# A recurrence and a two-layer network on one core: the first steps' instructions placed one by one, with six more idle products

## The chip, the cores and the metric

The kernel runs on one core of a Trainium2 chip. That core has TensorE (matrix products, PE in the profile), VectorE (DVE), ScalarE (ACT), GpSimd (POOL) and SyncE (SP), each with its own instruction queue; SyncE and GpSimd mostly issue transfers here. The metric is the device time of one execution in microseconds. Several executions of a kernel give a median.

## The reference

```python
# attention block: B, H, S, D = 4, 8, 768, 48
f = 1.0 / (1.0 + np.exp(-f_logit))
for t in range(S):
    state = f[:, :, t, :, None] * state + np.einsum('bhd,bhe->bhde', k[:, :, t], v[:, :, t])
    y[:, :, t] = np.einsum('bhd,bhde->bhe', q[:, :, t], state)
# x: y as (B*S, H*D) = (3072, 384)
h = x @ w_in                                            # 384 -> 2048
g = np.maximum(h, 0.0) + alpha * np.minimum(h, 0.0)
out = g @ w_out                                         # 2048 -> 384
```

A gated linear recurrence runs over 768 tokens for each of 4 x 8 heads; its output goes token by token through a two-layer network with a leaky gate.

## The kernel before, in words

The sequence is cut into six chunks of 128 tokens, and the four batches into two pairs. That makes twelve steps, numbered 0 to 11: step 0 is chunk 0 of the first pair, step 1 chunk 0 of the second, step 2 chunk 1 of the first, and so on. Each step has two halves. The attention half turns the recurrence of one chunk into products: it takes the sigmoid of the gates, makes running products of them, forms products of scaled queries and keys inside blocks of 32 tokens (in smaller parts: lags within four tokens, quads, halves), puts those masked into a matrix `A`, and multiplies by the values and by the state carried from the chunk before. The network half multiplies the step's 256 tokens (tile `xT`) by `w_in` (`ph`), gates the result, and multiplies by `w_out`.

In the attention half the names are these. `loaded` issues the loads of f, q, k and v, for step 0 on SyncE's queue and for all others on GpSimd's. `lagging` and `lagged_all` make the gates and the lagged copies `qd` (lines 329 to 346). `scanned` copies operands (lines 363 to 366), `scanned_all` runs two scans on VectorE (373, 374). `gated`, `keyed`, `started`, `ended`, `carried` and `begun` scale queries and keys (380 to 418). The products are `raw` (line 582, lags), `qu` (line 591 for quads, line 681 for the half blocks of steps 0 and 1), `off` (566, between blocks of 32), `pk` (713, transposes of the keys), `pd` (539, the state's increment), `py` (614, the output) and `xt` (738, which packs the output of step 0 into 128 rows). VectorE copies the masked parts of `raw` (599) and `qu` (702) into `ad`; ScalarE copies the rest (688), then `ad` into `A` (606), `off` into `A` (573), the keys (719), the increment (556), the output (729), and `xT` (747).

The weights arrive as 64-bit numbers in 16 pieces of some 767 KB on SyncE's queue. ScalarE takes each apart in two instructions (lines 281 and 282), VectorE puts the halves together in a third (291). The words `a0` to `a7` are the load and ScalarE's two instructions for a piece of `w_in`, `w0` to `w7` VectorE's instruction for it; `b0` to `b7` and `v0` to `v7` are the same for `w_out`. `W`, `Y` and `Z` with a number derive sums and splits of the weights for another form of the network, which later steps use.

In the first step TensorE also runs products whose result is not used: fourteen at the start (`IDLE`), six (`BEFORE`, words `0I0` to `0I5`) and eight (`BEHIND`, words `0J0` to `0J7`). The profile shows them at line 935, two records each.

The order of all this is written out by hand in `ORDER_WORDS`. A word names a step and a part: `0r1` is step 0, `raw` of the second batch of the pair; `0Na3` is step 0, network, product 3 of the first layer. A word that runs issues all the instructions of its part, on whatever engines they are for. In the kernel before, the order of words binds TensorE, VectorE and ScalarE; the queues of GpSimd and SyncE are ordered by the scheduler:

```python
    with tc.manual_schedule(engines={mybir.EngineType.PE, mybir.EngineType.DVE, mybir.EngineType.Activation}):
...
        for key in ORDER:
            run[key]()
```

## Time and profile before

| | us |
|---|---|
| median of 3 runs | 595.74 |
| lowest, highest | 594.69, 597.52 |
| span of the profiled execution | 592.1 |
| TensorE busy in that span | 580.1 |
| VectorE busy | 505.7 |
| ScalarE busy | 300.4 |
| GpSimd busy | 68.4 |

The profiled execution shows its span and no other time. In the profile PE is TensorE's products, PEld its weight loads (which overlap products), PEclk the clock that TensorE was granted (1.00 is full). A timeline's row gives the start from the beginning of the span, the duration, the engine, the line, and what is written from what; runs of equal instructions are put together (x128). In brackets is the idle time of the engine ahead of the row and what ended it. A row of windows gives the stretch, its length, each engine's busy time with its instructions, the clock, the share of the DMA engines, and GB/s.

### The profile page before, as it was taken

The numbers are of one execution on the slowest core, as the hardware profiler recorded it, in microseconds if no ns is written. First come the engines' busy times: TensorE is split into PE (matmuls) and PEld (weight loads), VectorE is DVE, ScalarE is ACT, GpSimd is POOL, SyncE is SP. The second block draws the span as 40 slices with busy tenths as digits, with TensorE's granted clock in tenths as the row PEclk, the third lists the DMA queues.
The fourth block names the chain that finished last, engine by engine and source line by source line (L and its number), as shares of the span: only waits on it lengthen the run. The fifth ranks groups of instructions, "written<-read, shape, count | busy, mean of one in ns | idle before, by whom it ended". The sixth has DMA issues, their size and how long they took to land.

```text
span 592.1 us, 18853 instructions
## 1 busy us (share of the span) xinstructions
PE 580.1 (98%) x8200; PEld 527.9 (89%) x8200; DVE 505.7 (85%) x1027; ACT 300.4 (51%) x561; POOL 68.4 (12%) x114
## 2 busy tenths in 40 slices
PE   8799999999999999999999999999999999999997
PEld 6678767899899999999999999899899999899997
DVE  7889799899999989899989889989989979966243
ACT  5697973461472473483382374374275355443230
POOL 9110010000101101111111101101100100100100
PEclk9689999999999999999999999999999999999999
DMA  9959212612523823724624614722732731611300
GB/s 299 356 160 348 98 22 63 172 30 86 123 86 91 191 78 89 172 65 105 169 60 106 153 68 106 164 74 85 148 110 81 152 110 54 112 44 30 80 2 27
DMA packets 69443, 67.57 MB, mean 114 GB/s; under 512 B 44688, under 2 KB 58640, under 8 KB 69360
## 3 DMA queue, kind: packets, MB, share of 16 engines
q1 hardware_dynamic: 59744, 37.16, 22.1%
q0 software_dynamic: 8880, 28.84, 19.2%
q8 instruction: 64, 1.05, 0.7%
q10 hardware_dynamic: 736, 0.37, 0.2%
q14 instruction: 19, 0.16, 0.1%
HBM read 44.99 MB, written 13.50 MB: 99 GB/s over the span
## 4 chain that ended last, share of the span: by engine, by line
PE 80%; issue 10%; DMA 4%; ACT 3%; DVE 3%; POOL 1%; POOLq 0%; ACTq 0%; DVEq 0%
PE ph L831 36%; PE pa L886 9%; PE pd L886 5%; PE pf L886 5%; PE pe L886 5%; PE pb L886 5%; PE pc L886 4%; PE py L614 3%; PE qu L591 3%; PE raw L582 3%; DMA w_out_raw<-in_w_out 2%; PE pd L539 1%; PE off L566 1%; DVE ad L451 1%; DMA f<-in_fT 1%
## 5 line engine op out<-in xcount | busy, mean ns | idle before, releaser
L831 PE MATMUL ph<-xT,w_in_sb 128*128 128x256 f32 x612 | 137.1, 380 | 0.2 <-DMA xT<-y 0.2
L831 PEld LDWEIGHTS ph<-xT,w_in_sb 128*128 128x128 f32 x612 | 115.1, 190 | 16.9 <-issue 0.9
L854 ACT ACTIVATE gate<-ph 128x512 f32<-128x512 f32 x96 | 54.6, 594 | 134.4 <-PE ph L831 127.5
L859 DVE SCALAR_TENSOR_TENSOR gate<-gate,om,ph 128x256 f32<-128x256 f32 x192 | 81.0, 476 | 25.6 <-ACT gate L854 25.1
L886 PE MATMUL pa<-w_out_sb,gate 128*128 128x192 f32 x352 | 61.7, 329 | 0.0
L880 DVE TENSOR_TENSOR gate<-gate 128x512 f32<-128x512 f32 x88 | 57.6, 690 | 3.2 <-PE pb L886 2.4
L886 PEld LDWEIGHTS pa<-w_out_sb,gate 128*128 128x128 f32 x352 | 57.1, 190 | 0.5
L599 DVE COPY_PREDICATED ad<-mraw,raw 128x256 f32<-128x256 int32 (+1 forms) x96 | 42.7, 445 | 8.9 <-PE raw L582 6.2
L451 DVE COPY_PREDICATED ad<-mquad,qu 128x224 f32<-128x224 int32 (+6 forms) x140 | 42.2, 302 | 6.8 <-PE qu L591 1.7
L606 ACT COPY A<-ad 32x256 f32<-32x256 f32 x96 | 38.7, 403 | 11.8 <-DVE ad L451 10.4
L440 DVE TENSOR_TENSOR scores<-scores,fs 128x768 f32<-128x768 f32 (+5 forms) x60 | 37.4, 623 | 1.6
L844 ACT ACTIVATE ph<-ph 128x512 f32<-128x512 f32 x36 | 20.2, 574 | 34.0 <-PE ph L831 25.2
L831 PE MATMUL ph<-xh,hi 128*128 128x256 f32 x216 | 34.4, 295 | 0.0
L831 PE MATMUL ph<-xl,lo 128*128 128x256 f32 x216 | 32.0, 283 | 0.3 <-issue 0.3
L886 PE MATMUL pb<-t,gate 128*128 128x192 f32 x176 | 31.2, 331 | 0.0
L831 PEld LDWEIGHTS ph<-xh,hi 128*128 128x128 f32 x216 | 28.7, 190 | 2.8 <-issue 1.6
L424 ACT COPY A<-q 48x512 f32<-48x512 f32 x44 | 27.2, 617 | 7.8 <-DVE q L398 7.2
L886 PE MATMUL pd<-t,gate 128*128 128x192 f32 x176 | 30.7, 328 | 0.3 <-DVE gate L880 0.3
L886 PE MATMUL pc<-t,gate 128*128 128x192 f32 x176 | 30.6, 327 | 0.0
L886 PE MATMUL pf<-w_out_sb,gate 128*128 128x192 f32 x176 | 30.5, 327 | 0.0
L323 POOL DMA_DIRECT2D vs<-in_v x22 | 13.2, 605 | 149.4 <-PE py L614 149.1
L886 PE MATMUL pe<-w_out_sb,gate 128*128 128x192 f32 x176 | 30.4, 326 | 0.0
(153 smaller groups left out, 1044.0 us busy)
## 6 DMA issues: line engine op xcount, KB each, us to landing
w_out_raw<-in_w_out SPq DMA_DIRECT2D x8, 767.8 KB, 9.6
w_in_raw<-in_w_in SPq DMA_DIRECT2D x8, 767.2 KB, 9.5
q<-in_qT POOLq DMA_DIRECT2D x11, 512.0 KB, 5.1
f<-in_fT POOLq DMA_DIRECT2D x11, 512.0 KB, 5.2
k<-in_kT POOLq DMA_DIRECT2D x11, 512.0 KB, 4.2
turned<-f SPq DMA_DIRECT2D x40, 128.0 KB, 4.4
ksn<-turned SPq DMA_DIRECT2D x10, 512.0 KB, 3.5
out<-o SPq DMA_DIRECT2D x24, 192.0 KB, 1.9
```

What stands on the lines that cost most here:

```text
L424: nc.scalar.copy(A[halves(cc)[1], :, par * HP:(par + 1) * HP, CH * cc:CH * (cc + 1)], x["q3"][rows(par)].rearrange("p (u h c) s t -> p u h ...
L440: nc.vector.tensor_tensor(by_four(us[:, :, UO[m]:UO[m] + 4 * n]), by_four(us[:, :, skip:skip + 4 * n]), spread(fq[:, :, 1:1 + n], n), ALU. ...
L451: nc.vector.copy_predicated(ad[:, u, :, :, 4 * m:DB], mquad[:, lo:lo + n].bitcast(I32).unsqueeze(1).unsqueeze(1).broadcast_to((128, 2, HP, ...
L582: nc.tensor.matmul(raw[DB * j:DB * (j + 1), par, hp * C:hp * C + QW], lhsT=x["k"][r_, g * DB:(g + 1) * DB], rhs=qd[r_, g], start=True, sto ...
L599: nc.vector.copy_predicated(adu[:, :, :, d:4], mraw[:, d, :, d:4].bitcast(I32).unsqueeze(1).broadcast_to((128, H, NB, n)), rv[:, :, QO[d]: ...
L606: nc.scalar.copy(A[s_, u, :, s_], ad[s_, u].rearrange("p r h t -> p (r h) t"))
L831: nc.tensor.matmul(banks[f][:, j * T:(j + 1) * T], lhsT=of[:, kt, 128 * j:128 * (j + 1)], rhs=by[:, kt], start=first_ and kt + j == 0, sto ...
L844: nc.scalar.activation(banks[f], banks[f], AF.Copy, scale=1.0 - 1.0 / EPS)
L854: nc.scalar.activation(to, of, AF.Relu, scale=-1.0)
L859: nc.vector.scalar_tensor_tensor(to[:, j], to[:, j], om[:, m:m + 1], of[:, j], ALU.mult, ALU.add)
L880: nc.vector.tensor_tensor(block(to)[:, p], block(x_)[:, p], block(y_)[:, p], op)
L886: nc.tensor.matmul(banks[to][:, 0:DH], lhsT=block(of)[:, f], rhs=of_w_out(by)[:, f], start=start and f == 0, stop=f == NH - 1, skip_group_ ...
```

## The change

Parts are no longer issued whole. Every part that has several instructions is a generator that yields between them, and a word in the order issues the next instruction of its part; a word therefore stands in the order as many times as its part has instructions. The loads are split into four words (`ef`, `eq`, `ek`, `ev`). GpSimd's and SyncE's queues are now bound to the order too. Tiles that used to be made when a part began are made when first used (`Later`).

With that the order of words is new. From about the middle of step 3 on, each engine's instructions stand in the order they had. (On GpSimd's queue single loads of f, q and k still swap places in later steps.) Ahead of that they are moved, without any being added or dropped but for six idle products (`BEFORE` 6 to 12). In steps 0 and 1 these moves are the ones to follow:

- SyncE: f, q, a piece of `w_in`, k, a piece of `w_out`, two of `w_in`, half of v, a piece of `w_in`, the other half of v, and further pieces. Before: f, q, k, v, v, and then pieces.
- TensorE: `raw`, eleven idle products (five before), `off`, `qu`, `pk`, three idle products, second `qu`, one, `pd`, two, `py`, one, `xt`, second `py`, one, `xt`, `raw` twice, `ph`. Before: `off`, `pk`, `qu`, and both `py` ahead of the first `xt`.
- VectorE: line 386 ahead of 380; the lags (599) of the first half of step 0 mixed in earlier; 663 and 664 ahead of the scaled keys (402, 406).
- ScalarE: eight instructions on weight pieces (six before) ahead of the copies of `off`; behind them the copies of lines 688, 719, 606 and 424, the sigmoid and copies of step 1 (329 to 331) and the copies of line 556 one by one in turn.
- Steps 1, 2 and part of 3: pieces of weights, lags, gates of the network and scans are mixed in another order on all engines; the list of products ahead of the first `ph` is the same but for the idle ones.

The new kernel calls the tile of line 539 `inc` instead of `pd`. The diff, cut to its core:

```diff
-IDLE, BEFORE, BEHIND = 14, 6, 8
+IDLE, BEFORE, BEHIND = 14, 12, 8
...
-0e 1e 0I0 0f 0F 0G 0g 0r1 0h 0i 0m 0p 0j 0r0 0I1 0l 0I2 a0 0R0 0I3 0I4 0I5 0q 0o a1 0k a2 0O 0s 0t w0 0u0 0U0 0R1
-0K0 0H0 1f 0J0 0J1 0J2 w1 0K1 0u1 0J3 0U1 1F 0A0 0d 0D 0H1 0A1 w2 1G 0J4 0J5 0y0 0Y0 b0 0J6 0y1 0x0 0Y1 0M 1g 1i 0J7
-1r0 0x1 1R0 0X a3 1h a4 b1 w3 a5 1m 1r1 w4 1j 0Na0 v0 0Nr0 0Na1 0Na2 1R1 0Na3 a6 0Nc0 w5 0Nr1 0Na4 0Na5 0Nc1 2e 0Nr2
...
+0ef 0f 0f 0eq 0F 0f 0F 0F 0I0 a1 0ek 0F 0F 0g 0g 0g 0g b0 a2 0F 1ef 0r1 a0 0r0 0g 0g 0I1 0G 0G 0I2 0i 0ev 1eq a1 0h b0
+0R0 0j 0m a2 0R0 a3 a2 0p 0p 0p 0p 0I3 0I4 0I5 0I6 0R0 0p 0ev b0 b2 0I7 0R0 0q a1 0q 0l 0I8 0I9 0I10 0I11 a0 a0 0o 0u0
+0l 0U0 0U0 0U0 a4 0O 0O 0s 0k 0s 0R1 0R1 0R1 0O 0J0 0O 0H0 0K0 0R1 0A0 0J1 0H0 0t 0K1 0A0 1ek b3 0J2 1f 0H0 0u1 0J3 1f
+0s b4 w2 v0 0U1 0A0 0U1 0H0 0U1 0t 0H1 0H1 0H1 0d w0 1f 0H1 0D 0A0 0D w1 0A1 0A1 0s 0A1 a5 0J4 2ef 1F 1F 1F 0J5 1F 1F
+0y0 0Y0 1F 0A1 0J6 0x0 0y1 0J7 0M a3 a3 0Y1 0x1 a4 0M a4 0X 0X 0M 1r0 w3 0X 1g 1G 1r1 a7 w4 1g 1p a5 0Na0 1i a5 a6 1g
...
+class Later(dict):
+
+    def __init__(self):
+        self.make = {}
+
+    def __missing__(self, key):
+        self[key] = self.make[key]()
+        return self[key]
+
+
+class Word:
+
+    def __init__(self, part):
+        self.part, self.left = part, None
+
+    def __call__(self):
+        if self.left is None:
+            got = self.part()
+            self.left = got if hasattr(got, "gi_frame") else iter(())
+        next(self.left, None)
...
         nc.scalar.activation(f, f, AF.Sigmoid)
+        yield
         nc.scalar.copy(kr[:, :, 2:3], f[:, :, 3:4])
-        nc.scalar.copy(qd[:, :, 0:DB], q.rearrange("p (g t) -> p g t", t=DB))
+        yield
+        nc.scalar.copy(qd[:, :, 0:DB], x["q"].rearrange("p (g t) -> p g t", t=DB))
...
         for j in range(NJ):
+            if j:
+                yield
             s_ = slice(DB * j, DB * (j + 1))
             nc.scalar.copy(A[s_, u, :, s_], ad[s_, u].rearrange("p r h t -> p (r h) t"))
...
-    with tc.manual_schedule(engines={mybir.EngineType.PE, mybir.EngineType.DVE, mybir.EngineType.Activation}):
+    with tc.manual_schedule(engines={mybir.EngineType.PE, mybir.EngineType.DVE, mybir.EngineType.Activation,
+                                     mybir.EngineType.Pool, mybir.EngineType.SP}):
...
+        run = {key: Word(part) for key, part in run.items()}
         for key in ORDER:
             run[key]()
```

## The prediction

> **What bounds the kernel now.** First the page: busy times, and the chain that ended last.

> ```profile
> span 592.1 us, 18853 instructions
> PE 580.1 (98%) x8200; PEld 527.9 (89%) x8200; DVE 505.7 (85%) x1027; ACT 300.4 (51%) x561; POOL 68.4 (12%) x114
> ...
> PE 80%; issue 10%; DMA 4%; ACT 3%; DVE 3%; POOL 1%; POOLq 0%; ACTq 0%; DVEq 0%
> ```

> TensorE is idle for 12.0 us of the whole span, and it carries the chain. An order of instructions can therefore gain only by closing those gaps, or by changing how long TensorE's own work takes. The second is possible because the granted clock (PEclk) is not full everywhere, as the view by windows shows (span, busy time of each engine with instructions, clock, DMA).

> ```profile
> 5.29:18.94 13.65, 9.75 (x227) 8.06 (x226) 11.51 (x20) 10.34 (x17) 11.24 (x23) 1.00 1.05 366
> 15.50:18.94 3.44, 0.93 (x66) 0.85 (x67) 3.41 (x9) 2.85 (x5) 1.89 (x3) 1.00 1.01 389
> 18.94:32.60 13.66, 13.66 (x242) 10.92 (x241) 11.15 (x26) 8.82 (x19) 0.73 (x1) 0.50 1.03 340
> 32.60:46.25 13.65, 12.33 (x240) 10.28 (x239) 11.68 (x18) 13.33 (x27) 2.65 (x4) 1.00 0.41 106
> 46.25:240.00 193.75, 192.82 (x2586) 167.84 (x2585) 180.13 (x353) 105.02 (x193) 16.07 (x23) 1.00 0.40 115
> ```

> From 18.94 to 32.60 TensorE had half the clock. The 13.65 us before that were 0.71 busy (9.75 of 13.65) and their last 3.44 us only 0.27; the half-clocked window was all busy and full clock came back; the next, 0.90 busy, kept it. From 46.25 to 240 TensorE is idle for 0.93 us in total, while VectorE is busy 180.13 of 193.75 us. So the place to read is the first 46 us; behind it a reordering has 0.93 us to win and a nearly full VectorE to stumble over.

> TensorE's timeline (start, duration, what; last the idle time before it):

> ```profile
> 10.70 1.59 PE L582 MATMUL raw<-qd,k 48*32 48x80 f32 x128 [0.53 <-issue]
> 12.22 2.43 PE L935 MATMUL idle<-ones 128*128 128x256 f32 x10
> 17.47 0.21 PE L566 MATMUL off_0a<-q,kh 48*32 48x32 f32 x1 [2.83 <-DVE kh L402]
> 20.55 1.05 PE L591 MATMUL qu<-scores,k 48*32 48x52 f32 x64
> 21.57 1.97 PE L681 MATMUL qu<-scores 48*128 48x64 f32 x16
> 23.47 2.93 PE L935 MATMUL off_0a<-ones 128*128 128x256 f32 x6
> 34.10 1.15 PE L614 MATMUL py<-A,vs 128*64 128x64 f32 x32 [0.78 <-ACT ad L688]
> 36.42 1.15 PE L614 MATMUL py<-A,vs 128*64 128x64 f32 x32 [0.54 <-ACT y L729]
> 37.50 1.60 PE L738 MATMUL xt<-y,dense 128*128 128x128 f32 x12
> 41.85 0.92 PE L582 MATMUL raw<-qd,k 48*32 48x80 f32 x64
> 42.70 8.04 PE L831 MATMUL ph<-xT,w_in_sb 128*128 128x256 f32 x36
> 58.34 1.04 PE L713 MATMUL pk<-ident,ks 128*128 128x128 f32 x8
> 65.37 0.82 PE L591 MATMUL qu<-scores,k 48*32 48x52 f32 x64
> 66.12 1.11 PE L681 MATMUL qu<-scores 48*128 48x64 f32 x16
> ```

> The first dense product of the network, `ph`, starts at 42.70, and from there TensorE is fed almost without a gap. So the gain is the time by which that first `ph` moves forward, if nothing stalls behind it. The last three rows are the same kinds of product at full clock: `qu` takes 1.11 instead of 1.97 (L681) and 0.82 instead of 1.05 (L591).

> **The change, part by part.**

> *Loads.* On SyncE's queue a 767 KB weight piece now goes ahead of step 0's `k`, and `v` behind three more pieces.

> ```profile
> 1.74 0.47 SPq L313 DMA_DIRECT2D k<-in_kT  x1
> k<-in_kT SPq DMA_DIRECT2D x1, 512.0 KB, 6.2
> ```

> `k` lands at about 1.74 + 6.2 = 7.9; a piece more at 366 GB/s is 2.1 us, so 10.0, and its first reader `raw` starts at 10.70 because it waits for VectorE. Cost 0, with 0.7 us of cover; without that cover at most 2.1 − 0.7 = 1.4. `v` is first needed by the products of line 539, past 25 us. On GpSimd's queue step 1's loads come as f, q, k, each still needed only after 25 us: 0. Later swaps of single loads on that queue cost nothing either: GpSimd and its queue have 1% of the chain.

> *Idle products.* Ten records (five products) took 2.43 us, 0.486 each. There are now eleven between `raw` and `off`, ending at 12.22 + 11 × 0.486 = 17.57; `off` started at 17.47. They fill the 2.83 us gap and delay `off` by 0.1 us at most. The window 5.29 to 18.94 then has 9.75 + 2.83 = 12.6 busy of 13.65, or 0.92, which is what kept the clock in the next window (0.90). I take it that the clock stays full through 18.94. The gap was 2.83 us and the clock still fell. [...]

> *Order up to `qu`.* VectorE's and ScalarE's rows:

> ```profile
> 12.57 1.23 DVE L380 TENSOR_TENSOR scores<-scores,f 128x1024 f32<-128x1024 f32 x1 [0.60 <-ACT scores L365]
> 17.33 0.69 DVE L402 TENSOR_TENSOR ks<-k,ss 128x512 f32<-128x512 f32 x1
> 18.54 1.87 DVE L599 COPY_PREDICATED ad<-mraw,raw 128x256 f32<-128x256 int32 x4
> 20.84 0.67 DVE L664 TENSOR_TENSOR scores<-scores 128x512 f32<-128x512 f32 x1
> 23.64 1.14 DVE L702 COPY_PREDICATED ad<-mhalf,qu 128x224 f32<-128x224 int32 x3
> 22.22 1.25 ACT L424 COPY A<-q 48x512 f32<-48x512 f32 x2 [2.64 <-DVE q L398]
> 24.87 1.06 ACT L688 COPY ad<-qu 16x128 f32<-16x128 f32 x4 [0.81 <-DVE ad L702]
> 25.95 1.06 ACT L329 ACTIVATE f<-f 128x1024 f32<-128x1024 f32 x1
> 27.48 0.65 ACT L330 COPY k<-f 128x256 f32<-128x256 f32 x1 [0.47 <-PE qu L591]
> 28.03 1.04 ACT L331 COPY qd<-q 128x1024 f32<-128x1024 f32 x1
> 29.10 0.58 ACT L719 COPY ksn<-pk_0b 128x512 f32<-128x512 f32 x1
> 29.58 1.64 ACT L606 COPY A<-ad 32x256 f32<-32x256 f32 x4
> 31.97 0.96 ACT L556 COPY vs<-pd 48x384 f32<-48x384 f32 x2 [0.76 <-PE pd L539]
> 35.78 0.58 ACT L729 COPY y<-py 128x512 f32<-128x512 f32 x1
> ```

> L386 moves ahead of L380 and fills the 0.60 us for which VectorE waited; the two `ks` products (17.33 to 18.54, 1.21 us) move behind the operands of `qu`. The last of these, L664, then ends at 20.84 + 0.67 − 0.60 − 1.21 = 19.7 instead of 21.51. The transposes `pk` now follow the first `qu`. Its L681 part runs from 19.7 and at full clock ends at 20.8; VectorE's three L702 copies (1.14) end at 22.0, against 24.78 before. ScalarE, which began on them at 24.87, can begin at 22.1: 2.8 us earlier. At half clock L681 takes 0.86 more, and it would be 22.9.

> *From there to `py`.* Now ScalarE sets the end, since its pieces are mixed so that it need not wait. What it does until the first `py` can be finished, by the starts of consecutive rows: eight L688 copies at 0.27 (2.2), two `ksn` at 0.48 (1.0), four L606 at 0.41 (1.6), two L424 at 0.63 (1.3), L329 1.1, L330 0.6, L331 1.1, two L556 at 0.48 (1.0): 9.7 in all, so 31.8, against 34.10 for `py` before. Its waits must be hidden for this. The later four L688 come some 6.2 us into the list (28.3) and need the second `qu`: on TensorE `pk` (1.04), three idle products (1.46) and `qu` (0.82 + 1.11) end at 25.3, and VectorE, which first finishes the lags of the first half and two weight pieces, copies them by about 27.5. Cover 0.8 us. At half clock `pk`, idle products and `qu` take 2.0 + 2.9 + 3.0 from 21.7, so `qu` ends at 29.6, the copies at 30.7, and the cover is gone: 2.4 us late, `py` at about 34.2 as before.

> *`py` to `ph`.* The first `xt` now stands between the two `py`. First `py` to 32.9; four more L606 and `y` (4 × 0.41 + 0.58) let the second start at 34.1 and end at 35.2. Behind its `y` copy ScalarE has two weight copies queued ahead (about 0.8 each from 34.1), so `y` ends at 36.4; then `xt` (1.60) to 38.0 and two `raw` (0.9 each) to 39.7. The first `ph` starts at about 39.7 instead of 42.70: −3.0. The three `xT` copies fit beside `raw`.

> *Behind `ph`.* Steps 1 and 2 issue the same instructions in another order, on all five queues; TensorE needs the same time for them. Between 46.25 and 240 there are 0.93 us of gaps: the reorder can win at most that; I take half, −0.5. Downwards the bound is that VectorE falls behind and all 3.0 are given back, or a little more. VectorE's cover is 193.75 − 180.13 = 13.6 us of idle time, which is why I take the first.

> **Sum.** −3.0 − 0.5 = −3.5 us. The profiled span was 592.1 and gives 588.6. The page shows no other time of that execution; the median of the three runs is 595.74 (594.69 to 597.52), 3.6 above the span, taken as constant: 592.2 us. The spread of those runs and the sum's roundings give 591.0 to 593.7 for this case. 0.5% is 3.0 us, about what a measurement of this kernel can tell from no change, so this case lies near the edge of "faster" (592.76).

> **The rivals.**

> 1. *The low clock moves instead of going* (slower). TensorE's work between 18.94 and 32.60 at full clock is, by the rows, the rest of `qu` 1.9, `pk` 1.0, six idle products 2.9, second `qu` 1.9, line 539 some 1.2 and part of `py` 0.9: 9.8 of 13.65, or 0.72. The window that lost the clock before had 0.71. If the share over 13.65 us decides, half clock comes from 32.60 to 46.25, on the path to `ph` and on `ph` itself, and decides from a share somewhere between 0.71 and 0.90. Price: with `py` and `raw` at 1.3 times (the ratio of L591) and `xt` and idle products at up to twice, the 7.1 us from 32.6 to `ph` grow by 2.4 to 5.8; `ph` starts at 42.1 to 45.5, and at half rate loses half of what is left to 46.25, 2.1 to 0.4. That is +4.5 to +6.2 on −3.5: +1.0 to +2.7, about 597.6. For it: 0.72 against 0.71. Against it: the end of the earlier window was only 0.27 busy, the new one's weak end is nearer one half, and its gaps (waits for ScalarE's copies before line 539 and `py`) are about 1 us each. [...]

> 2. *The clock falls where it did.* Then the path is that worked out at half clock: `py` at 34.2, and only the better tail (two `py` with `xt` between) remains, about −0.8: 594.9. For it: the share is an inference from three windows. Against it: 0.92 busy.

> 3. *A stall behind `ph`.* VectorE has 93% of its time taken from 46.25 to 240, the gate products need it, and weight pieces have been moved between them. If one gate or layer-2 operand comes late by 3 us once, or by 0.3 us ten times, the gain is gone: 595.7, and up to 2 us beyond it at 598. For it: 93%. Against it: TensorE's 0.93 us of gaps in that stretch under the same load.

> 4. *Nothing changes*, because ScalarE waits in its new list as much as before: 595. The `qu` part alone speaks against it.

> **How the numbers follow.** Clock kept and path shorter: 0.48, of which 0.35 beyond 0.5% and 0.13 within. The drop moves: 0.28, of which 0.20 within 0.5% and 0.08 slower than 598.7 (where a `ph` stall adds to it). Same drop or nothing: 0.10, within but for 0.02 faster. Stall behind `ph`: 0.14, of which 0.05 within and 0.09 slower, since a stall that is there at all can repeat. Faster 0.37, same 0.46, slower 0.17. The predicted time is that of the first case, 592.2. The range takes in rival 1 and most of rival 3: 590.5 to 599.0.

> **What will show it.** Right: full clock from 18.94 to 32.60 and behind it; no gap ahead of `off`; first L702 copies ending near 22; first `py` near 32; first `ph` near 39.7; TensorE's gaps after that below 1 us up to 240. Wrong: half clock in a 13.65 us stretch that reaches into `ph` (rival 1), half clock from 18.94 (rival 2), TensorE waiting for VectorE's gates or for weight pieces between 46 and 240 (rival 3), ScalarE idle for over 1 us between 22 and 32 (rival 4).

## The result and the profile after

The changed kernel took 605.57 us (median of 4 runs, 603.85 to 606.58), the kernel before 596.11 beside it: a ratio of 1.0161 (1.0134 to 1.0187). It is 1.6% slower, where 592.2 and a range up to 599.0 had been forecast. The profiled execution has a span of 604.7 us, 12.6 more than before. Some 3 of these 12.6 us belong to the two executions and not to the change: the medians differ by 9.5. Every time on record lies 1.7 to 2.0 us above its span, so the profiled execution of the kernel before took about 594 us (an estimate), less than any of its four runs.

The page of the changed kernel: busy times, granted clock in 40 slices, transfers of code, and the chain.

```profile
PE 586.1 (97%) x8212; PEld 533.6 (88%) x8212; DVE 500.9 (83%) x1027; ACT 301.2 (50%) x561; POOL 67.8 (11%) x114
...
PEclk9869899999999999999999989999999999999999
...
q8 instruction: 65, 1.06, 0.7%
...
PE 90%; DVE 4%; issue 2%; ACT 2%; DMA 1%; SPq 0%; DVEq 0%; ACTq 0%
```

TensorE still carries the chain. It is busy 6.0 us longer (2.6 of that are the new idle products: 5.01 for line 1051 below, 2.43 before) and idle 6.6 us longer. Where, its timeline shows:

```profile
11.41 1.58 PE L681 MATMUL raw<-qd,k 48*32 48x80 f32 x128 [1.20 <-DMA k<-in_kT]
12.92 5.01 PE L1051 MATMUL idle<-ones 128*128 128x256 f32 x22
18.57 0.81 PE L690 MATMUL qu<-scores,k 48*32 48x52 f32 x64
24.15 0.31 PE L690 MATMUL qu<-scores,k 48*32 48x52 f32 x11 [1.27 <-DVE f L504]
26.79 0.97 PE L690 MATMUL qu<-scores,k 48*32 48x52 f32 x53 [2.33 <-issue]
27.68 1.97 PE L793 MATMUL qu<-scores 48*128 48x64 f32 x16
33.29 0.41 PE L633 MATMUL inc<-vs,ksn 64*48 64x48 f32 x7 [1.12 <-issue]
35.63 1.98 PE L717 MATMUL py<-A,vs 128*64 128x64 f32 x32
45.42 5.45 PE L944 MATMUL ph<-xT,w_in_sb 128*128 128x256 f32 x24
70.66 0.57 PE L690 MATMUL qu<-scores,k 48*32 48x52 f32 x24 [2.75 <-issue]
342.15 0.87 PE L944 MATMUL ph<-xl,lo 128*128 128x256 f32 x6
352.49 0.33 PE L681 MATMUL raw<-qd,k 48*32 48x80 f32 x5 [3.09 <-issue]
358.75 0.76 PE L663 MATMUL off<-q,kh 48*32 48x32 f32 x64
452.27 0.30 PE L633 MATMUL inc<-vs,ksn 64*48 64x48 f32 x7 [0.90 <-issue]
```

The front went as forecast up to the first `qu`, but for `raw`, which started 0.7 us late; there is no gap ahead of `off`. Then TensorE stops five times in the middle of a group of small products, and the releaser of those stops is "issue": the profile shows no other engine and no data that it waited for. The same products in the kernel before give the loss stage by stage:

```profile
335.01 0.87 PE L831 MATMUL ph<-xl,lo 128*128 128x256 f32 x6
343.70 0.87 PE L831 MATMUL ph<-xl,lo 128*128 128x256 f32 x5 [0.35 <-issue]
347.35 0.76 PE L566 MATMUL off<-q,kh 48*32 48x32 f32 x64
```

The first `ph` is 2.7 us late (45.42 against 42.70). The `ph` from `xl` at 342.15 is 7.1 late: 4.4 more, of which the stop ahead of 70.66 is 2.75. The `off` at 358.75 is 11.4 late, 4.3 more, behind the stop of 3.09. The stop of 0.90 at 452 and small waits make the last 1.2.

Behind the three longest stops the clock fell as well, behind the first together with the wait of 1.27 us ahead of it. Windows of the changed kernel: ahead of each loss of clock the last 3.41 us, then the stretch at half clock (span, busy PE, clock, DMA).

```profile
22.43:25.84 3.41, 0.76 (x14) 1.00 1.02 371
25.84:39.49 13.65, 11.58 (x178) 0.50 0.59 228
66.80:70.21 3.41, 1.11 (x51) 1.00 0.96 338
70.21:77.04 6.83, 6.38 (x46) 0.50 0.17 65
350.10:353.52 3.42, 1.03 (x11) 1.00 0.02 5
353.52:356.93 3.41, 3.41 (x18) 0.50 0.59 156
```

The stretches at half clock in this trace are 13.65, 6.83 and 3.41 us long (but for one at the end of the span), so four, two and one times 3.41; the one in the kernel before was 13.66. Here the clock fell behind 3.41 us that were 0.22, 0.33 and 0.30 busy: a third busy was not enough to keep it.

**What the stops are.** Counting all records of TensorE in the trace from 0 (products, weight loads and its semaphore instructions), each stop of this kind, in both kernels, stands ahead of a record whose number is 193 plus a multiple of 256. The trace also has the packets of queue 8 (16 KB each), and TensorE goes on 1.2 to 1.5 us after one has landed.

```
kernel  goes on at  idle   record                packet of code
after     26.79     2.33     705 = 193 +  2*256   24.29 to  25.56
after     33.29     1.12     961 = 193 +  3*256   30.72 to  31.81
after     70.66     2.75    1985 = 193 +  7*256   68.05 to  69.18
after    352.49     3.09    9921 = 193 + 38*256  350.16 to 351.25
after    452.27     0.90   12993 = 193 + 50*256  449.42 to 450.83
before   208.66     0.69    5825 = 193 + 22*256  206.25 to 207.21
before   343.70     0.35    9921 = 193 + 38*256  341.32 to 342.27
```

No packet in the two traces begins before TensorE is some 297 records ahead of the place where it would stop, so I take the page to be asked for from there on. From there to the packet it took 3.0 us near 60 us in the kernel before, and 8.1 in the changed one; 2.4 near 340 before and 5.5 after. What else was on its way then differs:

```profile
57.45 0.73 POOL L369 DMA_DIRECT2D f<-in_fT  x1 [40.48 <-DVE ad L700]
58.17 0.72 POOL L369 DMA_DIRECT2D q<-in_qT  x1
58.89 1.80 POOL L386 DMA_DIRECT2D vs<-in_v  x3
60.68 0.73 POOL L369 DMA_DIRECT2D k<-in_kT  x1
61.41 0.60 POOL L386 DMA_DIRECT2D vs<-in_v  x1
60.00:75.00 15.00, 12.25 (x209) 10.01 (x198) 9.66 (x23) 9.63 (x16) 2.01 (x4) 0.84 0.77 250
```

In the changed kernel the load of step 2's `f` stands first on GpSimd's queue and waits 40.48 us for its buffer, with q, v and k behind it; then all are issued within 5 us, just as TensorE needs a page. Before, that stretch carried much less:

```profile
60.00:75.00 15.00, 15.00 (x211) 11.44 (x204) 11.44 (x27) 14.69 (x28) 0.00 (x0) 1.00 0.19 75
```

### The profile page after: what moved, and what is told of

Same layout as the page of the kernel before. It is cut to its first block, busy times and chain, and to the rows that moved or that the text cites. A ratio compares the mean times of both kernels' runs of the same rounds, so it can differ in the third digit from the quotient of the medians.

```text
span 604.7 us, 18873 instructions
## 1 busy us (share of the span) xinstructions
PE 586.1 (97%) x8212; PEld 533.6 (88%) x8212; DVE 500.9 (83%) x1027; ACT 301.2 (50%) x561; POOL 67.8 (11%) x114
## 3 DMA queue, kind: packets, MB, share of 16 engines
q8 instruction: 65, 1.06, 0.7%
## 4 chain that ended last, share of the span: by engine, by line
PE 90%; DVE 4%; issue 2%; ACT 2%; DMA 1%; SPq 0%; DVEq 0%; ACTq 0%
PE ph L944 38%; PE pa L1002 9%; PE pd L1002 5%; PE pf L1002 5%; PE pe L1002 5%; PE pb L1002 4%; PE pc L1002 4%; PE py L717 4%; PE po L982 4%; PE qu L690 4%; PE raw L681 3%; PE inc L633 2%; DMA k<-in_kT 1%; PE off L663 1%; DVE ad L700 1%
## 5 line engine op out<-in xcount | busy, mean ns | idle before, releaser
L700 DVE COPY_PREDICATED ad<-mraw,raw 128x256 f32<-128x256 int32 (+3 forms) x96 | 42.4, 444 | 13.3 <-PE raw L681 11.4
L543 DVE COPY_PREDICATED ad<-mquad,qu 128x128 f32<-128x128 int32 (+6 forms) x140 | 41.9, 301 | 5.7 <-PE qu L690 1.3
L407 DVE TENSOR_TENSOR qd<-qd,f 128x768 f32<-128x768 f32 (+2 forms) x36 | 27.2, 755 | 7.1 <-ACT qd L400 7.1
L690 PE MATMUL qu<-scores,k 48*32 48x112 f32 (+1 forms) x1536 | 26.0, 257 | 6.6 <-issue 5.1
L1002 PE MATMUL pd<-t,gate 128*128 128x192 f32 x176 | 30.7, 328 | 0.2 <-DVE gate L996 0.2
## 6 DMA issues: line engine op xcount, KB each, us to landing
f<-in_fT POOLq DMA_DIRECT2D x11, 512.0 KB, 5.5
q<-in_qT POOLq DMA_DIRECT2D x11, 512.0 KB, 5.9
k<-in_kT POOLq DMA_DIRECT2D x11, 512.0 KB, 4.6
ksn<-turned SPq DMA_DIRECT2D x10, 512.0 KB, 3.4
```

Of the source, the lines that this page charges most:

```text
L407: nc.vector.tensor_tensor(qdv[d], qdv[d - 1][:, :, :, 1:5 - d], f[:, :, 1:5 - d].rearrange("p (g i) r -> p g i r", i=NB), ALU.mult)
L543: nc.vector.copy_predicated(ad[:, u, :, :, 4 * m:DB], mquad[:, lo:lo + n].bitcast(I32).unsqueeze(1).unsqueeze(1).broadcast_to((128, 2, HP, ...
L690: nc.tensor.matmul(qu[DB * j:DB * (j + 1), par, hp * QS + 4:hp * QS + QL], lhsT=x["k4"][r_, g * DB:(g + 1) * DB], rhs=x["us"][r_, g, 4:QL] ...
L700: nc.vector.copy_predicated(adu[:, :, :, d:4], mraw[:, d, :, d:4].bitcast(I32).unsqueeze(1).broadcast_to((128, H, NB, n)), rv[:, :, QO[d]: ...
L1002: nc.tensor.matmul(banks[to][:, 0:DH], lhsT=block(of)[:, f], rhs=of_w_out(by)[:, f], start=start and f == 0, stop=f == NH - 1, skip_group_ ...
```

## The experiments

Ratios are to the kernel before in runs on the same chip (594.7 to 595.2 us). The theory is the one just told, late pages of code; rivals were the clock, the place of the page edges and the order of products.

**GpSimd's and SyncE's queues free.**

```diff
-    with tc.manual_schedule(engines={mybir.EngineType.PE, mybir.EngineType.DVE, mybir.EngineType.Activation,
-                                     mybir.EngineType.Pool, mybir.EngineType.SP}):
+    with tc.manual_schedule(engines={mybir.EngineType.PE, mybir.EngineType.DVE, mybir.EngineType.Activation}):
```

> The changed kernel with GpSimd's and SyncE's queues left to the scheduler again, as before the change. Late-code theory (TensorE stops at every 256th of its records when the 16 KB of code behind it come late, and they come late when loads of step data and weights are issued in one bunch just ahead of the request): q is ahead of f again on GpSimd's queue in the later steps, so the stall of 3.1 us at 352 falls under 1 us and the half clock behind it goes; the stall of 2.75 us near 70 shrinks if the loads of step 2 are spread again. 605.6 falls to 597 to 601. Rival (the six idle products move the page edges by 24 records and put one into two fast groups of products): both stalls stay, 604 to 607. Rival (order of products on TensorE alone): the same, 604 to 607.

Measured: 601.79, ratio 1.0130 (1.0097 to 1.0162). SyncE's first 20 transfers keep their order; GpSimd's do not. Its loads are spread again, and the stretch from 60 us has no stop:

```profile
41.50 1.19 POOL L386 DMA_DIRECT2D vs<-in_v  x2 [9.91 <-PE py L717]
49.71 0.73 POOL L369 DMA_DIRECT2D k<-in_kT  x1 [7.02 <-DVE ad L700]
56.84 0.73 POOL L369 DMA_DIRECT2D f<-in_fT  x1 [6.39 <-DVE scores L457]
60.00:75.00 15.00, 15.00 (x204) 11.31 (x204) 12.78 (x29) 12.83 (x24) 0.00 (x0) 1.00 0.36 118
```

The page asked for near 60 came after 2.0 us instead of 8.1. The other traces agree: it came after 6.3 to 8.1 us in the four kernels with GpSimd's queue bound, and after 2.0 to 3.9 in the ten with it free. The stop near 349 is 1.17. So the bunch made by GpSimd's order is the cause of the stop at 70. The total does not show it by itself: the intervals of the two ratios overlap. This profile has a stop of 4.0 us at 33.55, in line 633, in the same place as the 1.12 of the changed kernel.

**q ahead of f from step 6 on.**

```diff
-... 6ef ... 6eq ...
+... 6eq 6ef ...
```

(and so for steps 7 to 11)

> The changed kernel with one thing moved: from step 6 on the load of f stands behind that of q on GpSimd's queue, not ahead of it. Late-code theory: the stall at 352 (3.1 us) goes under 1 us and so does the 3.4 us of half clock behind it; all before 300 us stays as it is, the stall near 70 too. 605.6 falls by 3.5 to 5, to about 601. Rivals (page edges moved by the idle products; order of products): no change, 604 to 607.

Measured: 603.00, ratio 1.0140 (1.0122 to 1.0157). The stop near 350 stayed (2.80). q was now issued 8 us ahead of f, and the page came 5.1 us after it could have been asked for. The pairing of f and q is not what delays this page; that part of the theory falls.

**The changed kernel without the six idle products.**

```diff
-IDLE, BEFORE, BEHIND = 14, 12, 8
+IDLE, BEFORE, BEHIND = 14, 6, 8
```

> The changed kernel without the six new idle products, all else as it is. Rival (page edges moved by 24 records): the stalls near 70 and at 352 go, 597 to 600. Late-code theory: the stall at 352 stays over 1.5 us and that near 70 too, 603 to 607. Theory of the prediction on the clock: the gap ahead of off opens to 1 to 3 us, half clock from 18.9 on, and that alone moves the first ph by at most 2 us.

Measured: 601.21, ratio 1.0102 (1.0082 to 1.0122), clear of the changed kernel's interval. It fell between what the two theories had said. First `ph` at 41.79 against 45.42, and 0.9 us ahead of the kernel before in this one profile. The stop near 67 (2.65) and its half clock stay, as they must if GpSimd's queue makes them.

**Six more idle products in the kernel before; six tiny ones; and five wide ones.** The three take the edit apart: records and time, records alone (32x32 by 32x32), time alone (512 columns).

```diff
-IDLE, BEFORE, BEHIND = 14, 6, 8
+IDLE, BEFORE, BEHIND = 14, 12, 8
```

> The kernel before with six more idle products behind the five that stand ahead of off; nothing else. Theory of the prediction on the clock: full clock from 18.94 to 32.60, first ph about 1 to 2 us earlier, 594 to 595 against 596. Rival (page edges moved by 24 records): a stall of about 3 us near 345 with half clock behind it, 599 to 601. Late-code theory: no large stall near 345; at full clock the pages of the first steps are used up faster while weights are still being loaded, so a stall of 0.5 to 2.5 us may come between 20 and 34 and take the gain: 594 to 598.

```diff
+        nc.tensor.matmul(idle[0:32, 0:32], lhsT=ones[0:32, 0:32], rhs=ones[0:32, 0:32], start=True, stop=True)
```

> The kernel before with six products of 32x32 by 32x32 behind the five idle ones: 24 more records of TensorE as with six idle products, but next to no time, so the gap ahead of off stays over 1.5 us. If the cost of the six idle products is the place of the page edges: the stall near 345 grows from 0.6 to about 2 us and that near 441 from 0.1 to about 0.9, together 2 to 2.5 us; the front may move either way by 2; 596 to 599 against 594.7. If the cost comes from filling the gap: no change, 594 to 596.

```diff
+        nc.tensor.matmul(idle[:, 0:512].rearrange("p (a n) -> p a n", a=2), lhsT=ones[:, 0:128],
+                         rhs=ones[:, 0:256].unsqueeze(1).broadcast_to((128, 2, 256)), start=True, stop=True)
```

> The kernel before with its five idle products behind raw twice as wide (512 columns): the gap ahead of off is filled but no record of TensorE is added, so no page edge moves. Stalls near 345 and 441 as before (0.6 and 0.1). Theory of the prediction on the clock: full clock from 18.9 to 32.6 and a first ph 1 to 2 us earlier, 593 to 594 against 594.7. Late-code theory: at full clock the pages between 18 and 34 are used faster than they come beside the weights, a stall of 1 to 3 us there and half clock behind it: first ph as before or up to 2 us later, 595 to 597.

Measured: idle products 598.41, ratio 1.0064 (1.0043 to 1.0085); tiny ones 598.85, ratio 1.0064 (1.0047 to 1.0081); wide ones 595.92, ratio 1.0002 (0.9981 to 1.0023). The cost is the 24 records, not the time. In the timelines of the kernel with idle products (first fence) and that with tiny ones (second) the page edge now lies seven records of products ahead of the end of line 538's group, as it does in the changed kernel; with wide ones (third) it is where it was, ahead of a `py` that waits for ScalarE anyway.

```profile
33.13 0.41 PE L538 MATMUL pd<-vs,ksn 64*48 64x48 f32 x7 [2.51 <-issue]
44.64 3.72 PE L830 MATMUL ph<-xT,w_in_sb 128*128 128x256 f32 x16
```

```profile
32.96 0.30 PE L538 MATMUL pd<-vs,ksn 64*48 64x48 f32 x7 [2.81 <-issue]
44.22 4.15 PE L830 MATMUL ph<-xT,w_in_sb 128*128 128x256 f32 x18
```

```profile
33.25 1.54 PE L614 MATMUL py<-A,vs 128*64 128x64 f32 x32 [2.00 <-ACT ad L688]
42.76 5.45 PE L831 MATMUL ph<-xT,w_in_sb 128*128 128x256 f32 x24
6.51:20.17 13.66, 12.10 (x230) 1.00 1.05 367
16.76:20.17 3.41, 1.85 (x73) 1.00 1.03 390
20.17:27.00 6.83, 6.54 (x148) 0.50 1.04 307
```

The wide products also settle the clock: the 13.66 us ahead of the loss were 0.89 busy and it was lost all the same. Closing the gap ahead of `off` (0.60 us of the 2.83 are left) gained nothing: the first `ph` came at 42.76 against 42.70. Later stops differ from the forecast: the one near 345 was 1.79, 1.90 and 1.92 in the three, so there the 24 records are not the whole of it.

**A mixture.** No new idle products, the two queues free, and step 0's k ahead of the first weight piece.

```diff
-... 0I0 a1 0ek 0F ...
+... 0I0 0ek a1 0F ...
```

> The changed kernel without the six new idle products, with GpSimd's and SyncE's queues left to the scheduler, and with the load of step 0's k ahead of the first weight piece. If the costs found so far are the three parts of the loss: raw at about 10.7 instead of 11.4, no stall near 70, under 1.5 us near 345, first ph at 41 to 42, total 592 to 597 against 594.7. If the new order of instructions in steps 1 and 2 costs by itself: 598 or more.

Measured: 596.76, ratio 1.0028 (1.0006 to 1.0051). First `ph` at 41.12, 1.6 us ahead of the kernel before in this profile; no stop near 70. Undoing these three takes away 1.3 of the 1.6%; the place of `k` was not tried alone. What is left behind `ph` are stops for code (1.75 at 203, 1.19 at 346) and waits for gates in the stages whose order is new:

```profile
PE ph L943 <- issue: 2.9, 2, 1.8
...
PE pa L1001 <- DVE gate L974: 0.5, 1, 0.5
...
PE pb L1001 <- DVE gate L974: 0.4, 1, 0.4
```

**The mixture with wide idle products.**

```diff
-    run.update({(f"I{k}", 0): lambda: idled(idle, 0) for k in range(BEFORE)})
+    run.update({(f"I{k}", 0): (wide if k else lambda: idled(idle, 0)) for k in range(BEFORE)})
```

> The same with the five idle products behind raw twice as wide, so that the gap ahead of off is filled without a record more. Theory of the prediction on the clock: full clock past 18.9 and a first ph 1 to 2 us earlier than in the run without the wide products, 591 to 595. Late-code theory: the stall comes later instead, beside the weights, and the first ph is as late or later: 593 to 599.

Measured: 596.96, ratio 1.0026 (1.0010 to 1.0041). The clock was full to 26.4 us, and the first `ph` came at 42.11, 1 us later than without, in one profile each. Ahead of it are two stops of 1.4 and 1.5 us for code (18.70, 26.27); the run without has one of 1.7 (17.94). Again no gain from the clock.

**Groups of small products taken apart**, in the kernel before, in the changed one and in the mixture.

```diff
-... 6Na5 7u1 7r1 6Nq5 7A0 7R1 7U1 6Na6 ...
+... 6Na5 7u1 6Na6 7r1 6Nq5 7A0 7R1 7U1 ...
```

(and the off of step 4 behind the next dense product)

> The kernel before with two groups of small products taken apart: a product of the first layer (of step 6) between the qu and the raw of step 7 (near 341), and the off of step 4 behind the next dense product (near 208). Late-code theory: the page that was used up in 2.5 us there, and that in 3.2, now last 1 to 2 us longer, so the stalls near 345 (0.6 to 2.2 so far) and near 209 (0.5 to 1.8) mostly go: 1 to 2.5 us faster, 592.5 to 594 against 595. If those waits are not for code: no change.

```diff
-... 1u1 1K1 0Nc5 1u0 2f ... v3 0Np0 ...
+... 1u1 1K1 0Nc5 2f ... v3 0Np0 1u0 ...
```

> The changed kernel with the second qu of step 1 behind the first product of the second layer, so that the two groups of small products near 66 don't stand next to each other; the loads stay bunched. Late-code theory: the page lasts 3 to 4 us longer, the stall of 2.75 near 70 goes, and the half clock behind it: 4 to 5 us faster than the changed kernel, ratio to before 1.007 to 1.010. If only the bunch of loads decides: the stall stays over 2 us, ratio 1.015 to 1.017.

> The mixed kernel (changed order, no new idle products, GpSimd's and SyncE's queues free, k first) with qu and raw of step 7 and qu and off of step 4 taken apart by a product of the first layer each. Late-code theory: the stalls near 203 (2.1) and 346 (1.5) mostly go, 2 to 3.5 us faster than the mixed kernel, 593 to 595 against 595. If the order of steps 1 to 3 costs by itself in VectorE's gates: it stays above 596.

Measured: 596.25, ratio 1.0006 (0.9988 to 1.0024); 603.40, ratio 1.0130 (1.0097 to 1.0164); 599.88, ratio 1.0073 (1.0051 to 1.0095). In all three the stop that was aimed at went: those near 209 and 345, that near 70, those near 203 and 346. So a page edge in a slower stretch cost nothing there, even with the loads bunched. None was a gain of the size expected: the products that were put back are late for others. Waits of the kernel before with its groups apart, and the timeline of the changed kernel with them apart:

```profile
PE py L613 <- ACT A L572: 0.8, 1, 0.8
...
PE pd L538 <- DVE ad L450: 0.6, 1, 0.6
```

```profile
81.42 0.92 PE L681 MATMUL raw<-qd,k 48*32 48x80 f32 x64 [2.00 <-ACT ad L802]
```

The mixture was some 3 us slower by it, with intervals that touch. One product of the first layer, moved to step 4's `qu`, left a wait of 1.3 us for a gate; the rest the trace does not explain. Its first `ph` was at 43.83 in this profile, 2.7 us later than in the mixture's, though up to there both kernels have the same instructions in the same order; here half clock came a second time, from 32.34 to 39.17. So a first `ph` read from one profile can be off by some 3 us, and the leads of 0.9 and 1.6 us read above are not shown to belong to the new order.

**The new order only up to the first `ph`.** The mixture's words to there, then the old ones.

```diff
-... 0Na0 1i a5 a6 1g ...
+... 1h b1 b1 b1 1m b3 b3 v3 1j 0Na0 b4 b4 v4 0Nr0 0Na1 a5 ...
```

> The mixed kernel again, but with the new order only as far as the first ph; from there on the words of the kernel before in their own order, whole (the five weight pieces that are half done by then are finished first). If the new order of step 0 is worth about 1.5 us and that of steps 1 to 3 costs 2 to 3: first ph at 41 to 42, no waits for gates near 118 and 165, 592.5 to 594.5 against 595. If the gain at the first ph is taken back by whatever follows, in the old order too (code pages, weights): 595 or more.

Measured: 607.99, ratio 1.0204 (1.0171 to 1.0238). First `ph` at 43.38, not 41 to 42. The seam decides it: ScalarE waits for a weight piece that is finished there, the gates stand behind it, and `ph` waits 11.43 us for one at 65.44 (line 974).

```profile
54.23 0.88 ACT L336 ACTIVATE w_out_lead<-w_out_raw 128x768 f16<-128x768 bf16 x1 [6.44 <-DMA w_out_raw<-in_w_out]
```

Whether the new order of step 0 alone would win stays open. None of these kernels beats the kernel before.

## Why the prediction was wrong, point by point

- *"Idle products": failed.* They were costed by time, at 0.1 us. They do fill the gap and the clock holds through 18.94, as said; but they are 24 more records, which move every later page edge: 0.6% by the tiny products alone, and 1.0161 to 1.0102 when taken out.
- *The clock as a gain: failed.* The loss moved instead of going, as rival 1 had it, but to 25.84 to 39.49 and not to 32.60 to 46.25. The rule taken was wrong: 13.66 us that were 0.89 busy lost it in the run with wide products, and 0.90 had kept it; nor did the busy share of the last 3.41 us decide by itself (last section). Idle time moved along TensorE's path and the loss moved with it: 2.83 us ahead of 17.47 before, 1.27 and 2.33 ahead of 24.15 and 26.79 here. The first `ph` came at 45.42, inside rival 1's 42.1 to 45.5, but by luck: two stops for code (2.33 and 1.12), which the rival did not have, are in it.
- *"Loads": mis-sized in one term, failed in another.* k was to land at 10.0. It was issued at 2.49 instead of 1.74, behind the weight piece's issue, and took 8.8 us instead of 6.2 + 2.1, so it landed at 11.3 and `raw` started at 11.41, 0.7 late.

```profile
k<-in_kT SPq DMA_DIRECT2D x1, 512.0 KB, 8.8
```

  That lateness was not decisive: without the six products `raw` was nearly as late (11.12) and the first `ph` 3.6 us earlier than here. The wrong step was to price GpSimd's queue at nothing because it has 1% of the chain. Binding it put f at its head for 40.48 us and cost the stop at 70 with its half clock. The later swaps of f and q, undone by themselves, showed no clear cost (1.0140 against 1.0161, intervals that overlap).
- *"Order up to qu": right.* The half-block copies were to end at 22.0; with `qu` starting at 18.57 they ended at 21.66 (20.52 + 1.14 in the row below).

```profile
20.52 1.14 DVE L818 COPY_PREDICATED ad<-mhalf,qu 128x224 f32<-128x224 int32 x3
```

- *"From there to py": failed.* The second `qu` was to end at 25.3 and ended at 29.65: 1.27 us waiting behind VectorE's copies, which I had ahead of it on VectorE but not as its releaser, 2.33 for code, and half clock from 25.84. The 0.8 us of cover for ScalarE was gone, and `py` came at 35.63 instead of 31.8.
- *"Behind ph": failed.* The bound upwards was taken from VectorE's idle time. TensorE lost 9.9 us there, nearly all at page edges and the half clock behind them. Rival 3 had a stall at this place, but named gates and weights; its price (2 us beyond no gain) was a fifth of the 9.5 that the medians show.
- *"Sum": one term mis-sized.* The 3.6 us from span to median were taken as constant; all times on record lie 1.7 to 2.0 above their spans, and the rest is that the profiled execution lay below the median. This does not touch the direction.

What stays open: why the page near 345 came 3.7 to 5.5 us after it could have been asked for in the six kernels with the 24 records more and 2.4 to 4.0 in the eight without. The ranges overlap, each is one profile, and the order of f and q did not decide it. Open too is what the new order of steps 0 to 3 is worth by itself: the 0.3% of the mixture are what the runs leave of it.

## What to carry to other kernels

On a TensorE that is never idle, count instructions as well as time: groups like these (64 products in 0.8 us) used up a page of code in 2 to 6 us, and a page edge there became a stop of 0.90 to 3.09 us when the next page came late. Look for idle time released by "issue" in the middle of a group, and check whether such places lie a multiple of 256 records apart. Leave a load queue in an order in which each load can be issued as its buffer comes free; here one load that waited 40.48 us at the head turned the rest into a bunch.

## What was not expected of the hardware

- TensorE stopped, by my reading for its own code, at places that lie a multiple of 256 records apart, up to 4.0 us (line 633 at 33.55 with the queues free), although only 65 packets, 0.7% of the transfer engines' time, carried it in the changed kernel.
- 24 records of next to no time cost 0.6% of a kernel of 8,200 products, while 2.4 us of idle products without a record more cost nothing that could be measured.
- In the run with wide products a stretch with 1.85 of 3.41 us busy lost the clock; `off` and the transposes `pk` made up what was busy at its end. A stretch of the changed kernel with q ahead of f, 0.66 busy with 120 records of `qu` and no transpose, lost it too (first line below). And one that was only 0.42 busy, with seven records of idle products, kept it in the kernel before with its groups apart (second line). So the busy share of these 3.41 us did not decide by itself; what else counts stays open.

```profile
64.11:67.53 3.42, 2.27 (x120) 1.00 1.04 347
13.39:16.81 3.42, 1.42 (x7) 1.00 1.05 403
```
